# Retention, mixer and gated layers in one kernel: loads four steps ahead, stores a slot later, weights fetched one per item

## The chip, the cores and the metric

The kernel runs on one core of a Trainium2 chip. The core has TensorE (PE, the matrix engine), VectorE (DVE), ScalarE (ACT), GpSimd (POOL) and SyncE (SP); in this kernel SP issues every DMA, in the order in which they are written. The metric is the device time of one execution in microseconds (us), as the median of several runs. The profile shows one execution.

## The reference

Three layers follow one another on 8 sequences of 576 positions, all in float32:

```python
# 1. retention: q, k, v are [8, 8 heads, 576, 64]
gamma = 1.0 - 2.0 ** (-5.0 - np.arange(H))
Dmat = np.where(rel >= 0, gamma[:, None, None] ** rel[None], 0.0)    # rel = i - j
attn = np.matmul(scale * np.matmul(q, k.T) * Dmat, v)                # x is [8, 576, 512]
# 2. mixer
h = x.transpose(0, 2, 1) @ U @ V                                     # rank 32, along the sequence
u = x + h.transpose(0, 2, 1)
x = u + np.maximum(u @ w_ch1, 0.0) @ w_ch2                           # 512 -> 2048 -> 512
# 3. gated layer
x_prev = x shifted by one position
xk = mu_k * x + (1 - mu_k) * x_prev;  xr = mu_r * x + (1 - mu_r) * x_prev
out = sigmoid(xr @ w_r) * (np.maximum(xk @ w_k, 0.0) ** 2 @ w_v)     # 512 -> 1024 -> 512
```

## The kernel before

The 4608 positions (8 sequences of 576) are cut into 9 blocks of 512 columns. Every large product is made in the number format fp32r, of which one operand alone is not exact enough: each operand is split into a high and a low part (ACT copies the high part, DVE or POOL subtracts it), and PE makes three products, high by high, low by high and high by low. Pairs of products of halves are made in seven instead of eight (the Strassen-Winograd scheme), for which sums and differences of weight quarters and of data quarters are made ahead. Weights arrive as 64-bit floats and are converted on the chip by ACT (`high`, `low`) and DVE (`join`).

**Stage 1, retention, and the first half of the mixer.** 40 steps, 5 for each of the 8 sequences ("batches" below), work through the chunks of a sequence (`step_of`, L1218). A step scales the keys of the step after next on POOL (`scale_k`, L796), makes the retention products on PE (`products_of`: `inter` L867, `own` L886, and for the next step `scores` L834 and `gain` L908), leaves PSUM by DVE (L848, L933, L945, L962), and transposes the result (L972). What a step loads (`load`, L787 qk and L789 kv, 512 KB each) is fetched by `load_to` at its start. The low-rank products (L993) and the mixing product (`mix`, L1023, added to the data by DVE at L1027) follow some steps later; in the third step of a batch they are done between parts of the hidden blocks.

Between retention products PE makes "hidden blocks": u by `w_ch1`, 128 rows for one block of columns (`hidden_part`, L381, 3 parts of 4 matmuls; ACT's relu L387 and a store L392 follow). A hidden block needs one of nine small tiles and one of two PSUM banks.

Beside that, `slot()` runs jobs in stages, one stage per slot: the weights of later stages are loaded (L184, L221, L224), converted, summed, split (ACT L132 and L270, POOL L133 and L271) and stored to DRAM (L193, L277), and one entry of the list `sums` (L1168) is taken per slot: the first sums of `w_ch1` for the pair below (`first_sums`, L290: DVE L298 and L306 to L309, ACT L314, DVE L315, store L316).

Loads, weights and operands share the pool `big` of 35 buffers of 4 KB per partition; a load waits on SP until its buffer is free, and everything behind it on SP waits too. The order of work is written out by hand: every engine does its instructions in the order of the program.

At the end of the stage the last hidden blocks are made (L1271) while ACT and DVE make the operands of the pair (`operands`, a generator whose steps are taken by `next`).

**Stage 2, the first product of the last pair of blocks** (`first_group`, L1294 on, matmuls L1327, 8 groups of 7 products). Its sums come back from DRAM by `load_first` (L327), one group ahead, into the pool `big2` of 16 buffers. `tick` runs a slot four times in a group; the second weights 0 to 3 are converted in these slots (`second_weight`, loads L412, activations L100 and L104, casts L449).

**Stage 3, the second product** (`products`, matmuls L552): 64 items, 16 for each pair of blocks. An item loads its hidden rows four items ahead (`load_item`, L481 to L484), makes sums two items ahead (`sums_item`, L492 to L496, one stored at L494) and splits one item ahead (`split_item`, ACT L511, DVE L512). The second weights 4 to 7 were stored in stage 1 and are loaded by `load_second` (L466).

**Stage 4, the gated layer**, follows.

Of the kernel before, what the change touches and what calls it, by code (L numbers as in the profile page):

```python
# [9 lines left out]
F32 = mybir.dt.float32  # L10
F32R = mybir.dt.float32r
# [32 lines left out]
def retention_mixer_kernel(ctx: ExitStack, tc: tile.TileContext, io):  # L44
# [15 lines left out]
    def unit(pool, dt, nm):  # L60
        return pool.tile([128, 2, 512], dt, tag="unit", name=nm)
# [36 lines left out]
    def high(out, raw):  # L98
        w = raw.bitcast(U32).rearrange("p (n t) -> p n t", t=2)
        nc.scalar.activation(out, w[:, :, 1].bitcast(F32), AF.Prelu, scale=DOWN, alpha=NEGATIVE)  # L100

    def low(out, raw):
        w = raw.bitcast(U8).rearrange("p (n t) -> p n t", t=8)
        nc.scalar.activation(out, w[:, :, 3], AF.Copy, scale=TOP, bias=BELOW)  # L104
# [184 lines left out]
    def first_sums(g):  # L289
        got = {}  # L290

        def whole():
            got["x"] = [cv.tile([128, 512], F32, tag="cf", name="cf", bufs=5) for _ in range(2)]
            for i, x in enumerate(got["x"]):
                f = g + HF * i
                w, c = w1[f // 4], slice((f % 4) * 128, (f % 4 + 1) * 128)
                for k in range(2):
                    nc.vector.tensor_tensor(  # L298
                        x[:, 256 * k:256 * k + 256].rearrange("p (k n) -> p k n", n=128),
                        w.h[k][:, :, c].bitcast(F32), w.l[k][:, :, c].bitcast(F32), op=ALU.add,  # L300
                    )

        def sums():
            x, y = got["x"]
            a11, a12, a21, a22 = x[:, :256], x[:, 256:], y[:, :256], y[:, 256:]
            nc.vector.tensor_tensor(a22, a21, a22, op=ALU.add)  # L306
            nc.vector.tensor_tensor(a21, a11, a21, op=ALU.subtract)
            nc.vector.tensor_tensor(a11, a22, a11, op=ALU.subtract)
            nc.vector.tensor_tensor(a12, a12, a11, op=ALU.subtract)  # L309

        def part(i):
            x = got["x"][1 - i]
            y = unit(big, F32R, f"fs{g}_{i}")
            nc.scalar.copy(y[:, 0], x)  # L314
            nc.vector.tensor_tensor(y[:, 1], x, y[:, 0].bitcast(F32), op=ALU.subtract)  # L315
            nc.sync.dma_start(  # L316
                kept_1[g][:, i], y.bitcast(F32).rearrange("p l (s n) -> p l s n", n=256)
            )

        return [whole, sums, lambda: part(0), lambda: part(1)]  # L320

    fs = {}

    def load_first(g):
        for i in range(2):
            x = fs[g, i] = big2.tile([128, 2, 2, 256], F32R, tag="unit", name=f"fw{g}_{i}")
            nc.sync.dma_start(x.bitcast(F32), kept_1[g][:, i])  # L327

    wkp, wkq = {}, {}
# [74 lines left out]
    def second_weight(j, pool):  # L404
        raw, got = [], {}
        out = pool if j else big2

        def load():
            for i in range(2):
                r = big2.tile([128, 512], I64, tag="unit", name=f"w2raw{j}_{i}")  # L410
                f = j + 8 * i
                nc.sync.dma_start(r, io["moe_w_ch2"][f * 128:(f + 1) * 128, :])  # L412
                raw.append(r)

        def down():
            got["a"] = unit(big2, F32, f"w2a{j}")
            got["f"] = unit(big2, F32, f"w2f{j}")
            for i in range(2):
                high(got["a"][:, i], raw[i])
                low(got["f"][:, i].bitcast(U32), raw[i])  # L420

        def fill(i):
            f = got["f"][:, i]
            join(f, got["a"][:, i], f.bitcast(U32))

        def sums():
            x = got["s"] = big2.tile([128, 4, 256], F32, tag="unit", name=f"w2s{j}")
            f = got["f"]
            a11, a21, a12, a22 = f[:, 0, :256], f[:, 0, 256:], f[:, 1, :256], f[:, 1, 256:]
            s1, s3, s2, s4 = (x[:, i] for i in range(4))  # L430
            eng = nc.gpsimd
            eng.tensor_tensor(s1, a21, a22, op=ALU.add)
            eng.tensor_tensor(s2, s1, a11, op=ALU.subtract)
            eng.tensor_tensor(s3, a11, a21, op=ALU.subtract)
            eng.tensor_tensor(s4, a12, s2, op=ALU.subtract)

        def part(i, lo, eng):
            w = (wp, wq)[i]
            if j not in w:
                w[j] = [  # L440
                    out.tile([128, 4, 256], F32R, tag="unit", name=f"w2{'pq'[i]}{j}_{x}")
                    for x in range(2)
                ]
            if lo:
                src = got["s"][:, 2 * i:2 * i + 2]
            else:
                src = got["f"][:, :, 256 * i:256 * i + 256]
            h, l = (x[:, 2 * lo:2 * lo + 2] for x in w[j])
            nc.scalar.copy(h, src)  # L449
            eng.tensor_tensor(l, src, h.bitcast(F32), op=ALU.subtract)  # L450

        def parts(lo, eng):
            for i in range(2):
                part(i, lo, eng)

        return [
            load, None, down, lambda: fill(0), lambda: fill(1), sums,
            lambda: parts(0, nc.vector), lambda: parts(1, nc.gpsimd),
        ]

# [304 lines left out]
    with ExitStack() as st:  # L765
# [395 lines left out]
        jobs += [block_weight(j, big, io["moe_w_ch2"], kept_2, "s", True) for j in range(KEPT, HF)]  # L1161
        for at, job in zip((0, 2, 4, 6, 8, 10, 12, 14, 16, 17), jobs):
            waiting.insert(at, job)
        sums = [x for g in range(HF) for x in first_sums(g)]

        def load_to(n):
            while units and N - len(units) < n:
                load(*units.pop(0))  # L1168
# [46 lines left out]

        def step_of(i):
            b, p = seq[i]
            load_to(i + (4 if i < 2 * NC else 3))  # L1218
            if i + 2 < N:
                scale_k(*seq[i + 2])  # L1220
            for fn, args in first.pop(i, []):
# [47 lines left out]
        gen = operands(x1, 0, even, odd, "f")  # L1269
        next(gen)  # L1270
        while ready:  # L1271
            hidden(1)
            for _ in range(3):
                next(gen, None)
        for _ in gen:
            pass
# [12 lines left out]

    def tick():  # L1290
        ticks.append(0)
        slot(new=len(ticks) % 4 == 1)

    exits = []  # L1294

# [57 lines left out]

        exits.append(last)

    load_first(0)
    for g in range(HF):
        extra = {}
        if g + 1 < HF:
# [9 lines left out]
        first_group(g, 4 * (g % 2), extra)  # L1369
    while exits:  # L1370
        exits.pop(0)()
    for j in range(KEPT, HF):
        load_second(j, 0)
    for n, (q, h, j) in enumerate(ITEMS):
        if n + 4 < len(ITEMS):
            load_item(n + 4)
        if n + 2 < len(ITEMS):
            sums_item(n + 2)
        if n + 1 < len(ITEMS):
            split_item(n + 1)  # L1380
        if j > 5:
            load_rest(q, ((0, 3), (2, 1))[h][j - 6])
        if n >= len(ITEMS) - 4:
            load_hidden(n - len(ITEMS) + 4)
        if n == len(ITEMS) - 1:
            split_hidden(0)
        if n and n % 2 == 0 and n < 2 * (HF - KEPT) + 1:
            load_second(KEPT + n // 2 - 1, 1)
        products(n)
        slot()  # L1390
        for _ in range(2):
            if rest and j < NF // 2 - 1:
                rest.pop(0)()
# [272 lines left out]
```

## Time and profile before

| | |
|---|---|
| median of 3 runs | 1434.05 us (1430.72 to 1437.57) |
| profiled execution | 1433.46 us, span 1431.7 us |
| PE busy | 1352.3 us, 94% of the span, 10248 matmuls |
| DVE, ACT, POOL busy | 912.7, 678.3, 376.8 us |
| granted clock of PE, mean | 0.970 |
| DMA | 342.11 MB, mean 239 GB/s, 67.3% of the 16 engines' span |

Times count from the first instruction. Busy is the time in which an engine works on an instruction; the idle time before an instruction is put down to what released it. The granted clock is the share of TensorE's full clock, 2.4 GHz; 0.50 is its lower level, 1.2 GHz, and a value between is the mean of a stretch. The DMA share is the mean busy share of the 16 DMA engines.

### The profile page before, as it was taken

How to read it: one execution, taken by the hardware profiler on the slowest of the kernel's cores; microseconds unless marked ns; L12 is line 12 of the kernel's file. 1: busy time of each engine (PE TensorE's matmuls, PEld its weight loads, DVE VectorE, ACT ScalarE, POOL GpSimd, SP SyncE). 2: the span in 40 equal slices, each digit the busy share in tenths (PEclk: the TensorE clock that was granted, in tenths of full speed). 3: DMA queues.
4: the chain of work that ended last, by engine and by line, in shares of the span. 5: the costliest groups of instructions: out<-in, count | busy, mean ns of one | idle time of the engine just before them, and what ended most of it. 6: DMA issues, size and time to landing. Idle time of an engine off the chain costs nothing.

```text
span 1431.7 us, 26130 instructions
## 1 busy us (share of the span) xinstructions
PE 1352.3 (94%) x10248; PEld 1105.8 (77%) x10248; DVE 912.7 (64%) x1268; ACT 678.3 (47%) x1185; POOL 376.8 (26%) x317
## 2 busy tenths in 40 slices
PE   6999888898998979979999999999999999999998
PEld 4688766676776767768788888888888888888897
DVE  4544465545433145467979798888797788787753
ACT  5553444445433237644434444465455455465432
POOL 2340244243443004202222221211411403303312
PEclk8899999999999999999999999999999999999999
DMA  9666698889886357898969888589147066074172
GB/s 346 229 212 233 236 324 290 299 309 331 284 270 210 130 180 261 292 375 312 316 225 307 278 281 284 193 308 349 70 164 279 29 231 239 1 266 175 70 288 84
DMA packets 134827, 342.11 MB, mean 239 GB/s; under 512 B 16432, under 2 KB 29616, under 8 KB 134704
## 3 DMA queue, kind: packets, MB, share of 16 engines
q1 hardware_dynamic: 134704, 340.44, 67.3%
q8 instruction: 81, 1.33, 0.4%
q14 instruction: 42, 0.34, 0.1%
HBM read 232.38 MB, written 108.00 MB: 238 GB/s over the span
## 4 chain that ended last, share of the span: by engine, by line
PE 58%; DMA 2%; DVE 1%; ACT 1%; issue 1%; SPq 0%; POOL 0%; DVEq 0%; ACTq 0%
PE v L1511 14%; PE gc L552 6%; PE ga L552 6%; PE gd L552 6%; PE kd L1415 3%; PE kc L1415 3%; PE ka L1415 3%; PE gb L552 2%; PE kb L1415 2%; PE rd L1415 2%; PE rc L1415 2%; PE ra L1415 2%; PE fc L1327 1%; PE fa L1327 1%; PE fd L1327 1%; PE c L633 1%
## 5 line engine op out<-in xcount | busy, mean ns | idle before, releaser
L387 ACT ACTIVATE hs<-h 128x512 f32<-128x512 f32 x112 | 66.7, 597 | 179.8 <-PE h L381 174.6
L1467 POOL TENSOR_TENSOR vl<-m,vh 128x512 fp32r<-128x512 f32 (+1 forms) x40 | 47.6, 1192 | 310.2 <-ACT vh L1466 240.2
L796 POOL TENSOR_TENSOR kv<-kv,ktab 128x512 f32<-128x512 f32 (+1 forms) x40 | 38.4, 959 | 231.7 <-DMA kv<-in_kv 155.2
L511 ACT CAST sbh<-rb 128x1024 fp32r<-128x1024 f32 x64 | 67.3, 1052 | 50.3 <-PE gd L552 39.2
L1511 PE MATMUL v<-vh,wv_0u 128*128 128x512 f32 x288 | 88.7, 389 | 0.0
L1511 PE MATMUL v<-vh,wv_1u 128*128 128x512 f32 x288 | 88.6, 389 | 0.0
L512 DVE TENSOR_TENSOR sbl<-rb,sbh 128x1024 fp32r<-128x1024 f32 x64 | 85.1, 1329 | 3.8 <-ACT sbh L511 3.6
L511 ACT CAST sah<-ra 128x1024 fp32r<-128x1024 f32 (+1 forms) x64 | 53.5, 836 | 66.7 <-DVE ra L493 29.9
L512 DVE TENSOR_TENSOR sal<-ra,sah 128x1024 fp32r<-128x1024 f32 (+1 forms) x64 | 65.2, 1018 | 25.1 <-ACT sah L511 12.9
L1467 POOL TENSOR_TENSOR vl<-c,vh 128x512 fp32r<-128x512 f32 (+1 forms) x40 | 62.1, 1573 | 25.9 <-ACT vh L1466 25.9
L1027 DVE TENSOR_TENSOR xt<-mx,xt 128x256 f32<-128x256 f32 x64 | 28.7, 457 | 61.7 <-PE mx L1023 61.7
L315 DVE TENSOR_TENSOR fs<-cf,fs 128x512 fp32r<-128x512 f32 x16 | 14.7, 922 | 81.2 <-ACT fs L314 73.2
L848 DVE TENSOR_TENSOR pm<-up,dtab 128x512 f32<-128x512 f32 (+1 forms) x40 | 25.3, 633 | 64.3 <-PE up L834 58.7
L1511 PEld LDWEIGHTS v<-vh,wv_1u 128*128 128x128 f32 x288 | 54.1, 188 | 11.2
L1511 PEld LDWEIGHTS v<-vh,wv_0u 128*128 128x128 f32 x288 | 53.9, 188 | 11.0
L1466 ACT CAST vh<-m 128x512 fp32r<-128x512 f32 (+1 forms) x40 | 23.2, 579 | 75.3 <-DVE m L1465 75.3
L1511 PE MATMUL v<-vl,wv_0u 128*128 128x512 f32 x144 | 56.0, 389 | 0.0
L1511 PE MATMUL v<-vl,wv_1u 128*128 128x512 f32 x144 | 56.0, 389 | 0.0
L569 POOL TENSOR_TENSOR m<-m,ur 128x512 f32<-128x512 f32 x8 | 11.7, 1490 | 162.9 <-ACT m L566 162.9
L596 POOL TENSOR_TENSOR x<-x,ur 128x512 f32<-128x512 f32 x16 | 24.6, 1549 | 106.5 <-DVE x L592 51.5
L665 ACT ACTIVATE tp<-x2l,omu 128x511 f32<-128x511 f32 x72 | 50.9, 712 | 3.3 <-DMA x2l<-xb 3.3
L1465 DVE SCALAR_TENSOR_TENSOR m<-m 128x512 f32<-128x512 f32 (+1 forms) x40 | 44.8, 1119 | 1.4
(375 smaller groups left out, 3983.3 us busy)
## 6 DMA issues: line engine op xcount, KB each, us to landing
wk<-keys SPq DMA_DIRECT2D x80, 512.0 KB, 5.8
rb<-hp SPq DMA_DIRECT2D x64, 512.0 KB, 6.9
hp<-hs SPq DMA_DIRECT2D x112, 256.0 KB, 3.6
wr<-gates SPq DMA_DIRECT2D x40, 512.0 KB, 6.7
qk<-in_qk SPq DMA_DIRECT2D x32, 512.0 KB, 6.0
kv<-in_kv SPq DMA_DIRECT2D x32, 512.0 KB, 6.6
ra<-hp SPq DMA_DIRECT2D x32, 512.0 KB, 7.0
ur<-ub SPq DMA_DIRECT2D x18, 512.0 KB, 5.6
```

Of the source, the lines that this page charges most:

```text
L387: nc.scalar.activation(h, hps.pop((t, f)), AF.Relu)
L511: nc.scalar.copy(hi_, src)
L512: nc.vector.tensor_tensor(lo_, src, hi_.bitcast(F32), op=ALU.subtract)
L552: nc.tensor.matmul(group[g][p], l[:, col(p)], r, start=(h == 0 and j == 0 and i == 0), stop=(i == 2 and last), skip_group_check=True,)
L665: nc.scalar.activation(tp[:, 1:], x[:, :BT - 1], AF.Copy, scale=omu[:, j, k:k + 1])
L796: nc.gpsimd.tensor_tensor(k, k, ktab[:, p, :n].to_broadcast([128, n, NP, D]), op=ALU.mult)
L1027: nc.vector.tensor_tensor(u, ps[:, :n], u, op=ALU.add)
L1327: nc.tensor.matmul(ps[b], w(lo, i), x[:, i], start=(new and i == 0 and j == 0), stop=(i == 1 and j == 2), skip_group_check=True,)
L1415: nc.tensor.matmul(ps[b], l, r[:, i], start=(part == 0 and i == 0 and j == 0), stop=(i == 1 and j == 2), skip_group_check=True,)
L1465: nc.vector.scalar_tensor_tensor(x, x, 0.0, x, op0=ALU.max, op1=ALU.mult)
L1467: eng.tensor_tensor(l, x, h.bitcast(F32), op=ALU.subtract)
L1511: nc.tensor.matmul(vacc[t][o], w.part(lo, g, col(o)), x[:, i, :], start=(g == 0 and i == 0 and j == 0), stop=(g == NG - 1 and i == 1 and j ...
```

## The change

Five things are done. The retention fetch runs four steps ahead in all steps (before, three from the eleventh on). The store of a first sum becomes a stage of its own, a slot behind the stage that makes it, and the last store of a group shares its stage with the first sum of the next group, so that the list has 41 entries instead of 32. The first sums of group 0 come into the pool `big` and are loaded before the last three hidden blocks, and the operand generator takes a step behind each part of a block. A second weight is converted a word per stage (9 stages instead of 8), and a new one starts every 6 ticks instead of 4. The kept second weights are loaded one per item, the first halves in items 0 to 3 and the second in items 6 to 9.

```diff
@@ first_sums
         def part(i):
             x = got["x"][1 - i]
-            y = unit(big, F32R, f"fs{g}_{i}")
+            y = got[i] = unit(big, F32R, f"fs{g}_{i}")
             nc.scalar.copy(y[:, 0], x)
             nc.vector.tensor_tensor(y[:, 1], x, y[:, 0].bitcast(F32), op=ALU.subtract)
+
+        def store(i):
             nc.sync.dma_start(
-                kept_1[g][:, i], y.bitcast(F32).rearrange("p l (s n) -> p l s n", n=256)
+                kept_1[g][:, i], got[i].bitcast(F32).rearrange("p l (s n) -> p l s n", n=256)
             )
 
-        return [whole, sums, lambda: part(0), lambda: part(1)]
+        return [whole, sums, lambda: part(0), lambda: store(0), lambda: part(1), lambda: store(1)]
@@ load_first
-            x = fs[g, i] = big2.tile([128, 2, 2, 256], F32R, tag="unit", name=f"fw{g}_{i}")
+            x = fs[g, i] = (big2 if g else big).tile([128, 2, 2, 256], F32R, tag="unit", name=f"fw{g}_{i}")
@@ second_weight
-            for i in range(2):
-                high(got["a"][:, i], raw[i])
-                low(got["f"][:, i].bitcast(U32), raw[i])
+
+        def words(i):
+            if i == 0:
+                down()
+            high(got["a"][:, i], raw[i])
+            low(got["f"][:, i].bitcast(U32), raw[i])
...
-            load, None, down, lambda: fill(0), lambda: fill(1), sums,
+            load, None, lambda: words(0), lambda: words(1), lambda: fill(0), lambda: fill(1), sums,
@@ the list of first sums
-        sums = [x for g in range(HF) for x in first_sums(g)]
+        sums = []
+        for g in range(HF):
+            x = first_sums(g)
+            if sums:
+                before, begin = sums[-1], x[0]
+                sums[-1] = lambda before=before, begin=begin: (before(), begin())
+                x = x[1:]
+            sums.extend(x)
@@ step_of
-            load_to(i + (4 if i < 2 * NC else 3))
+            load_to(i + 4)
@@ the last hidden blocks
         while ready:
-            hidden(1)
-            for _ in range(3):
+            if len(ready) == 3:
+                load_first(0)
+            t, f = ready.pop(0)
+            for part in range(3):
+                hidden_part(t, f, part)
                 next(gen, None)
@@ tick
-        slot(new=len(ticks) % 4 == 1)
+        slot(new=len(ticks) % 6 == 1)
@@ ahead of the groups, and of the items
-    load_first(0)
...
-    for j in range(KEPT, HF):
-        load_second(j, 0)
@@ the items
-        if n and n % 2 == 0 and n < 2 * (HF - KEPT) + 1:
-            load_second(KEPT + n // 2 - 1, 1)
+        if n < HF - KEPT:
+            load_second(KEPT + n, 0)
+        elif n >= HF - 2 and n - HF + 2 < HF - KEPT:
+            load_second(KEPT + n - HF + 2, 1)
         products(n)
```

## Rows read from the trace of the kernel before

**Rows 1.** Windows: length; busy PE, PEld, DVE, ACT, POOL; clock, DMA share, GB/s.
```profile
136.00:202.60 66.60, 62.25 (x815) 49.63 (x809) 34.04 (x62) 30.94 (x59) 21.34 (x21) 0.95 0.76 267
202.60:277.30 74.70, 63.59 (x824) 51.07 (x819) 38.24 (x63) 33.37 (x65) 27.29 (x25) 0.93 0.85 297
277.30:348.80 71.50, 63.61 (x820) 50.92 (x813) 35.29 (x69) 31.19 (x60) 27.32 (x26) 0.93 0.87 309
348.80:419.00 70.20, 63.00 (x816) 50.85 (x808) 27.61 (x44) 32.43 (x62) 29.28 (x28) 0.93 0.84 296
419.00:471.40 52.40, 44.09 (x644) 35.53 (x637) 13.72 (x28) 14.60 (x30) 17.76 (x17) 0.90 0.64 218
...
609.60:650.00 40.40, 32.49 (x132) 25.72 (x131) 26.55 (x33) 16.70 (x19) 0.00 (x0) 0.92 0.98 380
650.00:1374.00 724.00, 722.46 (x3184) 596.88 (x3183) 586.09 (x714) 361.86 (x581) 176.61 (x116) 1.00 0.62 217
```

**Rows 2.** Windows of single retention steps, and of the fourth to second steps.
```profile
85.70:94.10 8.40, 8.40 (x180) 6.91 (x173) 3.42 (x7) 6.01 (x12) 4.88 (x4) 1.00 0.24 93
102.50:115.00 12.50, 12.50 (x196) 10.15 (x191) 6.21 (x13) 2.34 (x5) 1.46 (x2) 1.00 0.33 108
136.00:147.40 11.40, 11.39 (x188) 9.03 (x182) 8.15 (x18) 4.94 (x10) 0.80 (x1) 1.00 0.76 263
256.30:277.30 21.00, 21.00 (x274) 17.01 (x267) 9.94 (x18) 11.59 (x23) 5.71 (x4) 1.00 0.95 332
277.30:295.70 18.40, 13.73 (x188) 10.87 (x181) 5.46 (x14) 5.06 (x10) 8.01 (x9) 0.81 0.95 328
...
461.10:471.40 10.30, 10.30 (x130) 8.31 (x124) 2.38 (x5) 2.79 (x7) 0.00 (x0) 1.00 0.60 175
181.00:232.30 51.30, 46.38 (x619) 37.31 (x615) 27.14 (x46) 25.86 (x51) 21.59 (x20) 0.93 0.94 320
256.30:307.30 51.00, 46.14 (x620) 36.95 (x614) 23.70 (x48) 25.81 (x51) 17.28 (x15) 0.93 0.91 316
327.40:378.50 51.10, 46.29 (x624) 37.21 (x617) 24.48 (x36) 26.28 (x51) 19.90 (x17) 0.93 0.92 329
```

**Rows 3.** PE's waits from 140 to 460 us: total, times, longest (us).
```profile
PE dn L908 <- POOL kv L796: 17.5, 11, 2.7
PE up L834 <- DMA qk<-in_qk: 13.4, 6, 3.0
PE mx L1023 <- DVE xt L1027: 5.7, 2, 4.9
PE mx L1023 <- ACT xs L982: 2.1, 1, 2.1
```

**Rows 4.** SP's waits from 120 to 460 us.
```profile
SPq L316 <- DVE fs L315: 28.5, 11, 4.5
SPq L787 <- POOL wsl L271: 12.8, 2, 6.6
```

**Rows 5.** POOL's waits from 140 to 460 us.
```profile
POOL kv L796 <- DMA kv<-in_kv: 110.8, 15, 16.8
```

**Rows 6.** Timeline of PE, opening a batch: start, us, instruction, idle before it.
```profile
280.69 0.69 PE L834 MATMUL up<-qk 64*64 64x64 f32 x32 [2.77 <-DMA qk<-in_qk]
```

**Rows 7.** Timeline of PE at the end of the hidden blocks.
```profile
512.32 1.20 PE L381 MATMUL h<-uh,w_3h 128*128 128x512 f32 x4 [1.29 <-ACT hs L387]
...
528.60 0.80 PE L1327 MATMUL fc<-fht,fw 128*128 128x512 f32 x1 [5.00 <-DMA fw<-first]
```

**Rows 8.** Timeline of ACT there.
```profile
510.72 1.05 ACT L697 CAST fht<-xt 128x1024 fp32r<-128x1024 f32 x1 [3.57 <-DVE xt L701]
```

**Rows 9.** PE's waits from 530 to 608 us, stage 2.
```profile
PE fa L1327 <- ACT f L1333: 3.0, 2, 1.5
```

**Rows 10.** Timeline of SP at the first items.
```profile
615.93 4.66 SPq L466 DMA_DIRECT2D w2p<-second  x8
```

**Rows 11.** Timeline of PE at the fifth item.
```profile
635.11 0.80 PE L552 MATMUL ga<-sal,w2p 128*128 128x512 f32 x1 [6.20 <-DVE sal L512]
```

## The prediction

> **What bounds the kernel now.** I read the windows by stage first [rows 1]. From 650 us to 1374 TensorE (PE) works 722.46 of 724.00 us at the full clock of 2.4 GHz (granted 1.00), so nothing that the change does can shorten that part, and nothing won ahead of it is given back there: what ends earlier before 650 moves the end by as much. The losses lie ahead of it. One batch of the retention stage takes 66.6, 74.7, 71.5 and 70.2 us for batches 3 to 6, and the last one (four of its five steps) 52.4, at granted clocks of 0.90 to 0.95.
>
> Single steps give the measure [rows 2]. The step that opens a batch takes 11.4 us at clock 1.00 (136.0 to 147.4, 188 matmuls) and 18.4 us where it is disturbed (277.3 to 295.7, the same 188 matmuls, clock 0.81): PE idles 4.7 us in it and then runs for a while at 1.2 GHz, half of its clock. The second step of a batch has the same matmuls as the first (11.4). The third is the 12.5 of 102.5 to 115.0 with one more hidden block of 12 matmuls, 2.7 us at its pace: 15.2. The fourth and fifth together take 21.0. An undisturbed batch is so 11.4 + 11.4 + 15.2 + 21.0 = 59.0 us, and the four steps of the last, with fewer hidden blocks, 8.4 + 8.4 + 12.5 + 10.3 = 39.6. The five stretches last 335.4 us and hold 4 x 59.0 + 39.6 = 275.6 of work: 59.8 us are lost.
>
> The waits of PE in that stage say what is late [rows 3]: 17.5 us (11 times) for POOL's scaling of kv, 13.4 (6 times) for the qk transfer itself, 5.7 and 2.1 for the mixing product. The clock loss that follows each gap is not in these sums. POOL's scaling waits for its own transfer, 110.8 us [rows 5], and blocks POOL's queue meanwhile; the 4.9 us wait of a mixing product hangs on that too, by a DVE sum that needs a buffer which POOL frees. So the fetch of qk and kv, issued one step before use, comes some 3 us late about twice a batch ([rows 6] is one). SP's queue is the reason [rows 4]: it stands 28.5 us (11 times) before the stores of the first sums until DVE has made them, and 12.8 us (twice) before a qk load until POOL frees a buffer.
>
> **The change, part by part.**
>
> *Fetch one step earlier, stores a slot later.* No transfer is added in the stage: the same qk, kv and fs DMAs, each pair of loads moved up in SP's queue by one step (8 to 15 us) past that step's hidden stores, weight loads and weight stores; the fs stores go one slot back, so SP's 28.5 us go. A lead of one step covers every wait of [rows 3], whose longest is 4.9 us. Behind the loads on SP stand the hidden stores; POOL has its scaling ready a step early, and its splits, the stores that wait for them, and DVE's sums come sooner. The first sums now need 41 slots instead of 32 (5 per group, the last store joined with the next group's first sum) and run on into the last two batches, where the DMA has room (0.64 in the last stretch of [rows 1]).
>
> What is late next is the DMA. From a batch's fourth step to the second of the next its share is 0.94, 0.91 and 0.92 over 51.3, 51.0 and 51.1 us [rows 2], of which 43.8 are work (21.0 + 11.4 + 11.4). The best that a long stretch of this trace reaches is 0.98, from 609.6 to 650 us [rows 1]. At that the three stretches need 49.2, 47.4 and 48.0 us: 5.4 + 3.6 + 4.2 = 13.2 us of the loss stay. So 59.8 - 13.2 = 46.6. I take off 6 for the gap in batch 3 [rows 3] (PE on ACT xs, 2.1, with the clock loss after it), where ACT is busy with casts and no fetch is late. Value: **40 us**. Bounds: 59.8 if the extra lead carries the surplus into the light third steps, and below nothing if the buffers don't allow the lead (rivals).
>
> The Trainium skill, page "DMA: Bandwidth & Descriptors", section Specifications, gives a core's share of HBM as about 358 GB/s. By that rule batches 4 and 5 (297 x 74.7 = 22.2 MB and 22.1 MB) would need 62.0 and 61.7 us, the retention stage would give 48 instead of 40, and the item stretch below 2 us less than I put down: 1374 in all. The trace does not follow it: 380 GB/s in one stretch of [rows 1], and 320 to 329 at over 0.9 busy in those of [rows 2].
>
> *End of the hidden blocks.* PE waits 5.00 us for the first sums' transfer [rows 7], which is issued only after the last hidden store; now it is issued three blocks (8 us) earlier from the other pool, where PE needs nothing else. That gives 5.0. The finer interleaving of the operand casts with the three parts of a block works against it: ACT's cast of ft waits for DVE until 510.72 [rows 8], and the relu behind it already holds PE for 1.29 us [rows 7]. With one generator step per part instead of three per block, two further casts of 1.05 us come ahead of that same relu, and PE's wait there grows by 2.1. Sum: **3 us** (0 to 8).
>
> *Second weights made a word at a time, a new one every 6 ticks instead of 4.* PE waits twice for ACT, 3.0 us in all [rows 9], where two words (four activations) and two casts of the weight before fall in one tick. Now one word does. I take **2 us**; 0 to 3. The last weight starts at tick 19 and ends at 27 of 32, ahead of its first use: nothing is late.
>
> *Kept second weights one per item.* SP issues eight 512 KB loads at once, 4.66 us, and the fifth item's operands behind them [rows 10]; PE then waits 6.20 us for a difference of these operands [rows 11]. The clock of that stretch is 0.92 over 40.4 us [rows 1], so up to 3.2 us more are lost to it. The change puts the item's loads first and two weight loads behind them. Is the DMA then late? Four items with 2 x 0.52 MB of operands, 0.26 of store and 1.05 of weights move 9.4 MB, which at 380 GB/s takes 24.8 us against 21.8 of PE work (24 matmuls each, at 227 ns: 722.46 us over 3184): 3 us behind after four items, and operands are fetched two items (10.9 us) ahead of their sums. It is covered. The second halves go from items 2, 4, 6, 8 to items 6 to 9, where the first use is item 12. **8 us**; 0 to 9.4.
>
> Sum: 40 + 3 + 2 + 8 = 53. The profiled execution took 1433.5 us (span 1431.7), 0.6 under the median of the runs, 1434.05, so the forecast is **1380 us**.
>
> **The rivals.**
>
> *The buffers eat the lead.* The pool has 35 buffers, and by my count of the code 35 are held at some loads now; two more per step can't be had, so the load of step i + 3 has to wait for a buffer of step i. In the likely case that is one that PE frees within about 1 us of the step's start. For this rival speaks that qk loads already stand up to 6.6 us for POOL [rows 4]. If POOL's buffers are what is waited for, most of the lead goes; what stays is the 28.5 us off SP and the other three parts: 13 + about 8 = 21, so 1412.
>
> *Slower: SP held longer than the lead.* Same place, another price: everything that SP does is in order, so a held load holds the hidden stores, these hold the nine small tiles, these hold ACT's relu and PE's banks. It decides at a hold of about 11 us a step; at 13 us in some 20 steps it costs 2 us each, 40 in all, less 13 from the other parts: 1460. Against it: the two holds seen are 6.4 us on average, and an earlier kv ends POOL's 110.8 us of waiting, so POOL frees sooner.
>
> *The DMA is no limit.* The surplus drains in the light third steps and every loss goes, the gap in batch 3 too: 1433.5 - 59.8 - 13 = 1361.
>
> *Nothing changes* because another wait of the same size stands right behind each: against this speaks that undisturbed steps run at clock 1.00 with no gap [rows 2].
>
> **Chances.** Forecast 0.60 (its own range 1366 to 1396); buffers eat the lead 0.18; no DMA limit 0.08; slower 0.08; nothing 0.06. The range from 1362 to 1416 takes in the forecast, most of the first rival and a part of the third. Over 0.5% is 7 us, about what a measurement of this kernel can tell: faster 0.86, within it 0.06, slower 0.08.
>
> **What would show it.** PE's waits for POOL kv and qk under 5 us together in the retention stage; batches of 60 to 65 us; DMA share over 0.95 from fourth to second steps; no SP wait on the sums; POOL's wait for kv gone. At the end of the hidden blocks no wait for fw, but one of 3 to 4 us for a relu. No PE gap over 1 us at the fifth item. The prediction is wrong if qk loads wait on SP for POOL in most steps, or if PE waits for hidden relus in the retention stage.

## The result, and the profile after

The changed kernel takes 1443.41 us (median of 9 runs, 1438.67 to 1447.46), the kernel before 1434.05 in the same rounds: a ratio of 1.0063, interval 1.0045 to 1.0080. It is slower by 9 us, where 1380 was forecast. The profiled execution took 1441.68 us, its span 1439.9.

Windows of the profile after, batch by batch (length; busy PE, PEld, DVE, ACT, POOL with instructions; clock, DMA share, GB/s):

```profile
136.40:206.40 70.00, 61.81 (x820) 49.66 (x812) 32.74 (x57) 29.54 (x56) 22.54 (x21) 0.95 0.69 233
206.40:298.90 92.50, 67.13 (x808) 52.59 (x809) 32.60 (x58) 32.78 (x63) 27.62 (x25) 0.87 0.68 238
298.90:369.90 71.00, 63.87 (x804) 50.92 (x808) 38.52 (x61) 31.58 (x60) 31.71 (x30) 0.93 0.90 313
369.90:453.20 83.30, 64.50 (x820) 51.03 (x814) 33.52 (x61) 32.78 (x62) 25.57 (x24) 0.90 0.71 251
453.20:493.20 40.00, 40.00 (x652) 32.61 (x646) 14.64 (x29) 15.99 (x33) 17.29 (x16) 1.00 0.85 299
620.00:650.00 30.00, 27.90 (x113) 21.89 (x113) 22.06 (x27) 15.23 (x18) 0.00 (x0) 0.94 1.01 378
```

Against [rows 1] the last batch is what was forecast (40.0 us, no gap, clock 1.00; 52.4 before), and around the start of the items, at 630.8 us, PE works 27.90 of 30.00 us at a clock of 0.94 (last line above). But the batches before it take 70.0, 92.5, 71.0 and 83.3 us instead of 66.6, 74.7, 71.5 and 70.2. The five stretches last 356.8 us; before they lasted 335.4, and 295 was forecast. PE's waits in the retention and the last hidden blocks, 140 to 530 us, have changed altogether (total, times, longest):

```profile
PE h L383 <- ACT hs L389: 29.9, 8, 9.0
PE mx L1028 <- ACT xs L987: 12.7, 3, 8.1
PE mx L1028 <- DVE xt L1032: 10.6, 4, 6.7
PE up L872 <- ACT w L936: 3.1, 1, 3.1
PE up L872 <- DVE y L950: 2.5, 1, 2.5
```

The waits for qk and for POOL's kv of [rows 3], 30.9 us together, are gone. In their place PE waits for ACT: for the relu that ends a hidden block (29.9 us; 2.6 us in the same window before) and for the copy ahead of the mixing product (12.7 instead of 2.1). ACT's waits in the same stretch say why:

```profile
ACT wkf L104 <- POOL wkl L271: 15.9, 3, 8.9
ACT wsf L104 <- POOL wsl L271: 13.6, 2, 7.5
ACT fs L314 <- PE up L872: 7.8, 2, 5.3
ACT wsh L270 <- DMA first<-fs: 6.7, 2, 4.8
ACT wrh L270 <- PE up L872: 4.8, 1, 4.8
ACT fs L314 <- DMA second<-wsl: 4.8, 2, 4.5
```

In none of these does the releaser make what ACT reads. POOL's split wkl is no input of a conversion of the next weight; it is the last reader of the buffer that this conversion writes. Each line is a wait for one of the 35 buffers of the pool `big`. Summed over the conversions and splits of ACT (L104, L132, L270, L314, L370; those that write the small `cf` tiles left out) that waited for a store, for PE's last read or for POOL's split, it comes to 78.4 us in 23 waits. Before, the same sum is 2.4 us in 2:

```profile
ACT wv_0p L132 <- POOL wkl L271: 2.0, 1, 2.0
ACT fs L314 <- POOL wkl L271: 0.4, 1, 0.4
```

One wait of the changed kernel, followed through the timelines of SP, POOL, ACT and PE (start, length, instruction, idle before it and releaser):

```profile
218.19 0.34 SPq L792 DMA_DIRECT2D qk<-in_qk  x1
227.99 0.34 SPq L794 DMA_DIRECT2D kv<-in_kv  x1
230.29 1.13 SPq L277 DMA_DIRECT2D keys<-wkh  x2
...
236.54 2.48 POOL L271 TENSOR_TENSOR wkl<-wkf,wkh 128x512 fp32r<-128x512 f32 x2 [15.98 <-DMA keys<-wkh]
...
239.06 0.66 ACT L104 ACTIVATE wkf<-wkraw 128x512 uint32<-128x512 uint8 x1 [8.87 <-POOL wkl L271]
...
244.08 1.09 ACT L389 ACTIVATE hs<-h 128x512 f32<-128x512 f32 x2
...
244.74 1.65 PE L383 MATMUL h<-uh,w_2h 128*128 128x512 f32 x3 [8.99 <-ACT hs L389]
```

SP holds a kv load from 218.5 to 228.0 until PE frees a buffer; the store of wkh stands behind it. POOL's split waits 16.0 us for that store to free its buffer, ACT's conversion 8.9 us for the buffer that the split reads, two relus stand behind the conversion on ACT (after 4.4 us of other work that was held too), and PE idles 9.0 us. SP's waits after, 140 to 530 us:

```profile
SPq L794 <- PE up L872: 15.6, 2, 9.4
SPq L794 <- PE h L383: 14.7, 1, 14.7
SPq L184 <- ACT wkf L104: 13.1, 3, 5.2
SPq L794 <- DMA first<-fs: 9.1, 3, 4.0
```

The wait of the stores for DVE's sums [rows 4] is gone, as forecast; loads that wait for a buffer stand there instead, 63.3 us for all qk and kv loads (before 16.6). POOL's wait for its kv [rows 5] has fallen from 110.8 to 2.8 us.

Outside the retention it went as forecast. PE's timeline at the end of the hidden blocks and in the items:

```profile
536.21 1.20 PE L383 MATMUL h<-uh,w_3h 128*128 128x512 f32 x4 [3.51 <-ACT hs L389]
...
572.06 0.50 PE L1342 MATMUL fc<-fht,w_2h 128*128 128x512 f32 x1 [0.74 <-ACT f L1348]
...
602.67 0.50 PE L1342 MATMUL fc<-fht,w_3h 128*128 128x512 f32 x1 [1.50 <-ACT f L1348]
...
632.04 0.73 PE L557 MATMUL ga<-sah,w2p 128*128 128x512 f32 x2 [1.24 <-ACT sah L516]
```

The wait for fw [rows 7] is gone and the relu's has grown to 3.51 us. From that relu to the first item it is 98.1 us (532.7 to 630.8; before 511.0 to 615.3, 104.3), and from there to the end 809.1 (before 816.4): 6.2 and 7.3 us won. Up to that relu 21.7 us are lost.

### The profile page after: what moved, and what is told of

Its sections match the earlier page's. It is cut to its first block, busy times and chain, and to the rows that moved or that the text cites. A ratio compares the mean times of both kernels' runs of the same rounds, so it can differ in the third digit from the quotient of the medians.

```text
span 1439.9 us, 26131 instructions
## 1 busy us (share of the span) xinstructions
PE 1350.4 (94%) x10248; PEld 1103.1 (77%) x10248; DVE 915.8 (64%) x1268; ACT 677.3 (47%) x1185; POOL 379.8 (26%) x317
## 4 chain that ended last, share of the span: by engine, by line
PE 70%; DMA 5%; DVE 4%; ACT 2%; issue 2%; SPq 1%; POOL 1%; DVEq 0%; ACTq 0%; POOLq 0%
PE v L1525 13%; PE h L383 11%; PE gc L557 6%; PE ga L557 6%; PE gd L557 6%; PE kd L1429 3%; PE kc L1429 3%; PE ka L1429 3%; PE gb L557 3%; PE kb L1429 2%; PE rd L1429 2%; PE rc L1429 2%; PE ra L1429 2%; PE c L639 1%; PE c L638 1%
## 5 line engine op out<-in xcount | busy, mean ns | idle before, releaser
L517 DVE TENSOR_TENSOR sal<-ra,sah 128x1024 fp32r<-128x1024 f32 (+1 forms) x64 | 66.6, 1040 | 20.3 <-PE gd L557 12.2
L1032 DVE TENSOR_TENSOR xt<-mx,xt 128x256 f32<-128x256 f32 x64 | 28.7, 456 | 56.8 <-PE mx L1028 56.7
L383 PE MATMUL h<-uh,w_2h 128*128 128x512 f32 x112 | 35.2, 440 | 27.9 <-ACT hs L389 27.9
```

Of the source, the lines that this page charges most:

```text
L383: nc.tensor.matmul(hps[t, f], w.part(lo, k, fo), u[k // 2][:, k % 2, :], start=(part == 0 and k == 0), stop=(part == 2 and k == KD - 1),)
L517: nc.vector.tensor_tensor(lo_, src, hi_.bitcast(F32), op=ALU.subtract)
L1032: nc.vector.tensor_tensor(u, ps[:, :n], u, op=ALU.add)
```

## The experiments

**First question: which of the two retention edits costs?** Theory A: fetch and later stores together overfill the 35 buffers, so that ACT's own conversions wait for one and the relus behind them are late. Theory B: loads on SP wait for buffers and hold the hidden stores behind them. Theory C: what costs is the later stores and the 41 slots themselves. The letters are used again further down, with a meaning of their own in each group. Four kernels:

The change with the fetch of before:

```diff
-            load_to(i + 4)
+            load_to(i + (4 if i < 2 * NC else 3))
```

> The changed kernel with the fetch three steps ahead again; all else of the change stays. Theory A (buffers on ACT): the lead of four and the stores a slot later together hold more than the 35 buffers, so conversions on ACT wait for a buffer and the hidden relus behind them come late; without the lead the pool fits, PE's 29.9 us of waits for relus in the retention stage go, the fetch waits of before come back in part: about 1418 us (1410 to 1426). Theory B (buffers on SP): loads that wait for a buffer hold the hidden stores on SP, and those the relus; here too they go: about 1420. Theory C (stores and first sums): the stores a slot later and the 41 slots of sums bunch the work of ACT and DVE; the relu waits stay: 1440 or more.

1437.72 us, ratio 1.0015 (0.9999 to 1.0032). SP's waits for DVE's sums are gone here too, and the fetch is still late. PE's waits, 140 to 530 us:

```profile
PE up L839 <- DMA qk<-in_qk: 17.0, 5, 6.0
PE dn L913 <- POOL kv L801: 10.9, 7, 1.9
```

The kernel before with the fetch alone:

```diff
-            load_to(i + (4 if i < 2 * NC else 3))
+            load_to(i + 4)
```

> The kernel before with the fetch four steps ahead in all steps as the only edit. Theory A: the loads exceed the pool and wait on SP for buffers of their own step, but hardly an allocation on ACT does; the waits for qk and kv go and few relu waits come: 1400 to 1425. Theory B: SP is held by the loads as in the changed kernel, relus late: 1445 to 1460 (the changed kernel without the gains at the end of the stage and in the items). Theory C: no stores moved, so the lead gives all it can: about 1393.

1419.03 us, ratio 0.9891 (0.9855 to 0.9927).

The kernel before with two buffers of `big` held through the retention; DVE sets one column of each at the start and the end:

```diff
+        held = [unit(big, F32, f"held{k}") for k in range(2)]
+        for x in held:
+            nc.vector.memset(x[:, 0, 0:1], 0.0)
         for i in range(N):
             step_of(i)
+        for x in held:
+            nc.vector.memset(x[:, 0, 0:1], 0.0)
```

> The kernel before, fetch three ahead, with two of the 35 buffers held idle through the retention stage. Same number of free buffers as with the lead of four, without the lead. Theory A: few allocations on ACT exceed 33, loads come a little later: 1436 to 1448. Theory B: the loads on SP wait and hold the stores: 1445 to 1465. Theory C: the pool does not matter: 1434 within 4.

1460.94 us, ratio 1.0184 (1.0147 to 1.0221): 25 us for two buffers, with nothing else moved. That lies in theory B's range and 13 us above theory A's, but the trace has the waits where theory A puts them: ACT's waits for a buffer are 39.7 us (2.4 in the kernel before), SP's at qk and kv loads 14.4 us (16.6).

The change with each store back in its part's stage, and so 32 entries:

```diff
-        return [whole, sums, lambda: part(0), lambda: store(0), lambda: part(1), lambda: store(1)]
+        return [whole, sums, lambda: (part(0), store(0)), lambda: (part(1), store(1))]
...
-        sums = []
...
+        sums = [x for g in range(HF) for x in first_sums(g)]
```

> The changed kernel with each store of a first sum back in the stage of its part and 32 entries in the list; the fetch four ahead, the end of the stage, the ticks and the items as changed. Theory A: without the later stores ACT's allocations fit again; the lead works: 1385 to 1412. Theory B: the loads still wait on SP: 1436 to 1448, as the changed kernel. Theory C: 1380.

1401.61 us, ratio 0.9775 (0.9744 to 0.9806): it beats both kernels. The later stores, with the 41 entries that came with them, cost 41.8 us beside the fetch of four. Theory B, for which the fetch alone should have lost and this kernel too, falls. Theory A holds for the second and fourth kernel; it misses the first by 20 us (the store edit costs with a fetch of three, too) and puts the price of two buffers in the third too low.

**Second question: is it the later store or the longer list?** Theory H says the longer hold, theory S the spacing of the entries. First, 33 entries with each store a slot later; then, 41 entries with each store in its part's stage:

```diff
-        return [whole, sums, lambda: part(0), lambda: store(0), lambda: part(1), lambda: store(1)]
+        return [whole, sums, lambda: part(0), lambda: (store(0), part(1)), lambda: store(1)]
```

```diff
-        return [whole, sums, lambda: part(0), lambda: store(0), lambda: part(1), lambda: store(1)]
+        return [whole, sums, lambda: (part(0), store(0)), lambda: None, lambda: (part(1), store(1)), lambda: None]
```

> The changed kernel, but the list of first sums has 33 entries instead of 41: each store still goes a slot behind its part, the first store of a group shares a slot with the second part, the second store with the next group's first sum. Theory H (what costs is that each sum holds its 4 KB buffer, and its place in SP's queue, a slot longer): near the changed kernel, 1428 to 1445 us. Theory S (what costs is the spacing of 41 entries, which puts DVE's long sums at other places of the steps and runs them on into later batches): near the kernel with the store in its part's stage, 1396 to 1412.

1413.67 us, ratio 0.9859 (0.9839 to 0.9880).

> The changed kernel with its 41 entries, but each store issued in its part's stage and an empty stage where the store was; the sums and parts stand at the same slots as in the changed kernel. Theory H: near the kernel with the store in its part's stage, 1396 to 1412 us. Theory S: near the changed kernel, 1428 to 1445.

1415.67 us, ratio 0.9875 (0.9849 to 0.9902). Neither theory alone: from 1401.6 the later store costs 12.1, the spacing 14.1, both 41.8. They don't just add; together they cost 15.6 more.

The kernel with 32 entries and the stores with their parts is called the short-list kernel from here. It was run with the fetch of before, so that only the three parts behind the retention are left of the change, and with one empty entry ahead of the list:

```diff
-            load_to(i + 4)
+            load_to(i + (4 if i < 2 * NC else 3))
```

```diff
-        sums = [x for g in range(HF) for x in first_sums(g)]
+        sums = [lambda: None] + [x for g in range(HF) for x in first_sums(g)]
```

> The kernel before with only the edits behind the retention: group 0 of the first sums loaded before the last hidden blocks, a word of a second weight per stage, the kept second weights one per item. My sum had 3 + 2 + 8 = 13 us for these: 1421 (1418 to 1425). Theory H and theory S both say so; if it comes out at 1434 or above, the loss of the fetch-of-three kernel does not lie in the store edit at all.

1417.84 us, ratio 0.9886 (0.9865 to 0.9907): 17.2 us for the three parts (13 forecast). The fetch of four is then worth 16.2 (1417.8 to 1401.6), and 17.0 on the kernel before.

> The kernel with the store in its part's stage (four entries per group), with one empty entry ahead of the list: every first sum stands one slot later, so that DVE's four long additions go to the other half of a step; nothing is held longer. Theory H: as without the shift, 1397 to 1407 us. Theory S (the place of the sums in the step decides): 10 us or more away from 1401.6, either way.

1412.57 us, ratio 0.9854 (0.9830 to 0.9878). Shifted by one slot, with nothing held longer by the code, the list costs 11 us. That spoke for theory S; the traces show what the shift does: ACT's first sums wait for a buffer there, 16.5 us for the store of the sum before and 6.6 for PE.

**Third question: loads or places of work?** Theory P: the early loads take the buffers. Theory Q: the places of DVE's and ACT's work decide. Fetch moved behind the products of a step, in the changed and in the short-list kernel; and the four long additions of a first sum cut into two and two:

```diff
-            load_to(i + 4)
...
             products_of(i)
+            load_to(i + 4)
...
-        def whole():
+        def whole(i):
...
         def sums():
+            whole(1)
```

> The changed kernel, but the fetch of step i + 4 is issued behind the products of step i instead of at its start: a lead of about three and a half steps, with a buffer of step i freed ahead of it in the program. By a count of the code the loads that find all 35 buffers held fall from 22 to 6, those of conversions and splits stay. Theory P (the pool: loads of the long lead take or wait for the buffers that conversions need): 1405 to 1425 us. Theory Q (the places of the DVE and ACT work of the first sums in a step decide, whatever the pool): 1432 to 1447.

1443.28 us, ratio 1.0055 (1.0035 to 1.0076).

> The kernel with the store in its part's stage, and the fetch of step i + 4 behind the products of step i: no load finds all 35 buffers held any more by the count (17 before), 13 splits and conversions still do. Theory P: faster than 1401.6 us, 1385 to 1398. Theory Q: 1398 to 1406.

1404.12 us, ratio 0.9778 (0.9743 to 0.9813).

> The kernel with the store in its part's stage, and the four long additions of a first sum (6.3 us of DVE in a row at one place of the trace, ahead of the retention's own work) cut into two of 3 us, the second two with the four short ones of the next stage. Theory P: within 4 us of 1401.6. Theory Q: 1385 to 1397.

1405.41 us, ratio 0.9792 (0.9766 to 0.9819).

> Both: fetch of step i + 4 behind the products of step i, and the long additions halved, with the store in its part's stage. If both theories have a part, below each of the two: 1378 to 1392 us; if only one, as that one.

1403.49 us, ratio 0.9782 (0.9754 to 0.9811). All four stand within 4 us of the kernel that they start from. Theory P misses the first two, theory Q the third: moving the loads, or halving DVE's long additions, changes nothing here. That doesn't clear the pool, since the first two left its waits as they were: in the changed kernel the count of held buffers in program order fell for the loads from 22 to 6, but SP's loads waited 65.6 us for buffers (63.3 without the move) and ACT 75.0 (78.4). Such a count is a poor guide.

**Fourth question: the wait for a buffer on ACT (theory B here), or the slots (theory C)?** On the short-list kernel: one buffer held as above; each first sum's buffer kept two slots longer by a DVE write of one column, its store where it was; and the weight jobs started four in nine slots, there and in the changed kernel (the calls of `keep`, two entries behind each part, are left out below):

```diff
+        def keep(i):
+            nc.vector.memset(got[i][:, 0, 0:1].bitcast(F32), 0.0)
```

```diff
-                    slot(new=len(quiet) % 2 == 1 or len(quiet) > 40)
+                    slot(new=len(quiet) % 9 in (1, 3, 5, 7) or len(quiet) > 40)
```

> The kernel with the store in its part's stage, with one of the 35 buffers of the pool held idle through the retention (DVE sets one column of it at the start and at the end); nothing else is moved. Theory B (what costs is a conversion on ACT that waits for a buffer, with the hidden relus queued behind it): ACT's waits for buffers grow and the time with them, 1412 to 1435 us. Theory C (the slot at which the first sums' work and stores stand): within 5 us of 1401.6.

1456.29 us, ratio 1.0154 (1.0118 to 1.0189): one buffer of 35 costs 54.7 us, more than theory B said and far from theory C. ACT's waits of that kernel, 140 to 530 us, look like those of the change, though its list and stores are the short ones:

```profile
ACT wkf L104 <- POOL wkl L271: 20.9, 3, 8.7
ACT wsf L104 <- POOL wsl L271: 15.5, 2, 9.4
...
ACT wv_1p L132 <- DMA gates<-wrh: 8.1, 1, 8.1
ACT wv_1p L132 <- PE up L872: 5.8, 1, 5.8
```

and PE's longest wait in it is again for the relu:

```profile
PE h L383 <- ACT hs L389: 40.1, 8, 10.5
```

> The kernel with the store in its part's stage and 32 entries, but each first sum's buffer kept two slots longer by a DVE write of one column behind its store; the store itself stays where it is in SP's queue. Theory B: like the kernel whose 33 entries store a slot later, 1409 to 1422 us. Theory C (there it was the store's place in SP's queue): 1399 to 1406.

1413.62 us, ratio 0.9855 (0.9826 to 0.9885): what the later store costs with 33 entries (1413.67), without moving a store. SP's waits for DVE's sums are 39.0 us here and 0.7 with 33 entries, at the same time. So the hold is what costs there, and neither the store's place in SP's queue nor SP's wait.

> The changed kernel, all of it, but the weight jobs of the retention start four in nine slots instead of one in two, so that fewer of their buffers are held at a time and the last jobs end in the last batch; by the count of the code the conversions on ACT that find all buffers held fall from 14 to 5. Theory B: ACT's waits for buffers and PE's for relus fall, 1408 to 1430 us. Theory C: first sums and stores stand where they stood, 1436 to 1448.

1420.40 us, ratio 0.9908 (0.9873 to 0.9943), in theory B's range: 23 us back, with first sums and stores where the change has them.

> The kernel with the store in its part's stage, with weight jobs starting four in nine slots: no conversion on ACT finds all buffers held by the count (6 before). Theory B: faster than 1401.6 us, 1384 to 1397. Theory C: 1398 to 1407.

1411.51 us, ratio 0.9842 (0.9808 to 0.9876): a miss for both, 10 us slower than the short-list kernel. The other spacing makes ACT's first sums meet buffers that come free late (L314 waits 12.0 us for PE and 12.2 for stores); ACT's sum rises from 29.8 to 43.6 us. Like the kernel before with two buffers held, this run tells ACT's waits from SP's: its loads wait on SP no longer than those of the short-list kernel (15.2 against 17.8 us). But the weight jobs' work stands at other slots in it too.

**A better version.** The weight blocks' stores treated as the first sums' are in the short-list kernel, each in the stage of its split; and then the additions halved as well:

```diff
-            load, None, down, lambda: fill(0), lambda: fill(1), sums, lambda: parts(0),
-            lambda: store(0), lambda: parts(1), lambda: store(1),
+            load, None, down, lambda: fill(0), lambda: fill(1), sums,
+            lambda: (parts(0), store(0)), lambda: (parts(1), store(1)),
```

> The kernel with the first sums' stores in their part's stage, and the weight blocks' stores treated the same way: each is issued in the stage of its split and not a slot behind, so that two stages and the slots for which two pairs of buffers are held go. By the count of the code 33 buffers are held at most conversions and loads instead of 34 and 35, and 8 of them find all 35 held instead of 30. Theory B: ACT's waits for buffers fall, 1385 to 1398 us, less if SP's added waits for POOL's splits (1.3 to 1.7 us each) hold the hidden stores: up to 1408. Theory C: 1395 to 1410, by the new slots of the jobs.

1402.53 us, ratio 0.9794 (0.9767 to 0.9822), which lies in the ranges of both theories and decides nothing between them. ACT's waits for buffers fell to 13.3 us, of which these are most, and SP's for POOL's splits, which the edit was to add, came to little (waits of ACT, then of SP):

```profile
ACT wv_1p L132 <- DMA first<-fs: 4.9, 2, 2.6
ACT wv_0p L132 <- DMA first<-fs: 3.7, 2, 3.3
...
SPq L277 <- POOL wkl L271: 6.9, 12, 0.8
SPq L277 <- POOL wsl L271: 5.4, 10, 1.1
```

Its median is not below that of the short-list kernel, and its runs spread more (1396.3 to 1406.5).

> All stores of the stage issued with their parts, and the four long additions of a first sum (now 3.8 us of DVE in a row ahead of the retention's own work, behind which PE waited 5.9 us for a mixing sum) cut into two and two. Theory B says nothing of it: 1397 to 1407 us. Theory C (the place of DVE's work): 1385 to 1396.

1395.58 us, ratio 0.9734 (0.9711 to 0.9756): the fastest, 38 us under the kernel before. Its interval overlaps that of the short-list kernel (0.9744 to 0.9806), so that its lead over that one is likely and not shown. It came out in theory C's range, with its interval below that of the kernel without the halving (0.9767 to 0.9822), though single runs of the two overlap. So the place of DVE's additions, which was worth nothing in the short-list kernel, is likely to be worth some 7 us once the pool has room.

**All together.** For each kernel with the fetch of four and the three later parts, from 140 to 530 us: ACT's waits for a buffer (summed as above), SP's waits at qk and kv loads, and the median:

| kernel | ACT, us | SP, us | median, us |
|---|---|---|---|
| all stores at once | 13.3 | 5.1 | 1402.5 |
| all stores at once, additions halved | 15.4 | 6.3 | 1395.6 |
| short list, additions halved | 26.5 | 19.1 | 1405.4 |
| short list, fetch mid-step, additions halved | 28.3 | 17.2 | 1403.5 |
| short list, fetch mid-step | 28.9 | 18.7 | 1404.1 |
| short list | 29.8 | 17.8 | 1401.6 |
| short list, one slot on | 42.9 | 29.1 | 1412.6 |
| short list, slower jobs | 43.6 | 15.2 | 1411.5 |
| 33 entries, stores later | 45.4 | 40.1 | 1413.7 |
| 41 entries, stores with parts | 46.8 | 27.5 | 1415.7 |
| the change, slower jobs | 48.2 | 33.2 | 1420.4 |
| short list, kept two slots longer | 48.5 | 37.8 | 1413.6 |
| the change, fetch mid-step | 75.0 | 65.6 | 1443.3 |
| short list, one buffer held | 76.5 | 72.7 | 1456.3 |
| the change | 78.4 | 63.3 | 1443.4 |

From 29.8 us up the time goes with ACT's waits: some 0.9 us for each us of them (from 29.8 to 78.4 it is 41.8 us for 48.6). Between 42.9 and 48.5 us on ACT the time stays within 9 us, while SP's holds run from 15.2 to 40.1. Below 29.8 us it goes with them no longer (13.3 us at 1402.5). In the three slowest kernels SP's holds are high as well, 63 to 73 us, and no run parts the two there. The waits are those of the profiled execution, which for the first two rows took 1396.3 and 1402.8 us and not the median.

PE's side of the sum: between the profiled executions of the change and of the short list (spans 1439.9 and 1402.2) PE idles 28.7 us more and works 9.0 us longer on the same 10248 matmuls (busy 1350.4 against 1341.4, mean granted clock 0.970 against 0.977).

## Why the prediction was wrong

**The step that failed** is the first of the part by part, the stores a slot later: "the fs stores go one slot back, so SP's 28.5 us go", with no price on the other side. The wait on SP did go, but the fetch came no earlier for it: in the change with the fetch of before, PE still waits 27.9 us for qk and kv (29.0 in the three later parts alone). In the short-list kernel the wait is back at 20.7 us (12 times), while PE waits for no fetch. What the edit buys it with is one slot more for each of 16 sums' buffers, and with the 41 entries another order in which buffers come free. In a pool with none to spare the two together cost 41.8 us: 12.1 for the later store, which the kernel with the longer hold shows, 14.1 for the spacing, which goes with 17 us more of ACT's waits, and the rest where they meet. I had counted that 35 of 35 were held "at some loads", and looked for the price at the loads alone; ACT's conversions take their buffers from the same pool, and the relus queue behind them.

**The second failure is a size.** The fetch a step earlier, with the stores, was put at 40 us, and alone it gives 16 to 17. The first half of its mechanism is right: the qk and kv waits are gone in every kernel with it. But the lead takes two buffers more, and ACT's waits rise from 3.2 to 29.8 us (the three later parts alone against the short list), so that PE waits for relus and mixing sums instead. PE's waits of the short-list kernel, 140 to 530 us:

```profile
PE h L383 <- ACT hs L389: 23.4, 9, 7.0
PE mx L1028 <- DVE xt L1032: 8.1, 3, 5.6
PE mx L1028 <- ACT xs L987: 6.5, 2, 4.0
```

The next limit was to be the DMA, with 49.2, 47.4 and 48.0 us for the fourth to second steps. The same stretches of the short-list kernel:

```profile
184.00:238.20 54.20, 45.91 (x618) 36.41 (x612) 29.33 (x45) 25.61 (x50) 26.24 (x23) 0.94 0.91 312
260.70:314.40 53.70, 45.81 (x622) 36.30 (x616) 26.62 (x45) 25.80 (x51) 22.04 (x20) 0.94 0.95 325
331.70:379.60 47.90, 45.14 (x624) 36.38 (x618) 20.82 (x37) 26.72 (x51) 24.65 (x23) 0.96 0.99 351
```

Only the third comes to its forecast, at a share of 0.99. In the first two what PE waits for is ACT's relus alone (8.3 and 7.9 us), at shares of 0.91 and 0.95. The forecast's ceiling was also read too low, as the last section shows, and the slowest of the three stretches of [rows 2] moves 316 GB/s, not 320. The gap in batch 3, for which 6 us were left out of the gain, stayed (3.8 us in the change, 4.0 in the short-list kernel).

**What held.** End of the hidden blocks and second weights: 3 + 2 forecast, 6.2 measured between the two traces, with the relu's wait at 3.51 us where 3 to 4 was said. In part that is luck: of the 6.2 us only 3.8 are idle time of PE, and 2.4 are busy time saved at the higher clock (0.97 before, 1.00 after), which the forecast did not count; the wait for the second weights fell only from 3.0 to 2.2 us, where a gain of 2 was forecast. Kept second weights one per item: 8 forecast, 7.3 measured, the gap at the fifth item gone. The three parts alone came to 17.2 us in the medians against 13; in that kernel's own trace the spans give 2.4 us up to the last relu, 4.2 to the first item and 8.6 behind it, 15.2 in all. POOL's wait for kv [rows 5] fell as said.

**The rivals.** "Slower: SP held longer than the lead" named the end of the chain rightly, relus and then PE, and the sign; so did the last sentence of the prediction, that it is wrong if PE waits for hidden relus. Its road was only half right. Held loads on SP do start single chains, as the one shown, but over the kernels the time goes with ACT's own waits, and two runs have these without the holds on SP. Its time, 1460, was too high by 17, and it had been given a chance of 0.08. "Buffers eat the lead" was wrong in its price: the lead was there (no qk or kv wait), and the buffers took it elsewhere.

**What stays open.** The change with the fetch of before is 20 us slower than the three later parts alone (1437.7 against 1417.8), with ACT's waits up by only 15.8 us (3.2 to 19.0); part of it stands in waits of ACT for the small buffers of the sums, 14.4 us, which were not tried by themselves. PE's waits are 8.8 us longer there; those ahead of mixing products alone grow from 8.2 to 17.7 us. How the later store and the spacing come to cost 15.6 us more together was not tried either. And the kernels were compared with waits summed in one execution each; which single buffer costs most was not tried.

## What to carry to other kernels

Before moving a store back by a slot to spare a queue a wait, ask what the buffer that it frees is worth: in a pool without spare, one buffer of 35 cost 55 us here, and a wait of SP for a store's data, 39.0 us or 0.7, made no difference. Read the waits of every engine that allocates from a full pool, not only of the one that loads: here each releaser that is no producer of the instruction's input was a wait for a buffer, and what matters is what stands behind it in that engine's order. And price two edits that draw on the same pool together: the later store and the longer list cost 12 and 14 us apart, together 42.

## What the runs showed that was not expected

The forecast took 380 GB/s [rows 1] as the best that the transfers of a long stretch reach. But that is the mean of 40.4 us whose start is slower: from 620 to 650 us the kernel before already moves more (first line, columns as above), and the kernel with the three later parts alone does so while PE has no gap at all (second line):

```profile
620.00:650.00 30.00, 23.80 (x96) 19.22 (x95) 17.73 (x21) 10.00 (x10) 0.00 (x0) 0.89 1.03 412
620.00:650.00 30.00, 30.00 (x134) 24.86 (x133) 21.05 (x23) 12.83 (x17) 3.66 (x3) 1.00 1.03 413
```

The Trainium skill, page "Perfetto Trace Analysis", section "Roofline", says that the 358 GB/s which the prediction weighed is the share of a core when both cores of a pair draw on it, and that one core alone can go above it, to about 435. With one core at work this case's 413 agrees.

The same page of the Trainium skill, "Perfetto Trace Analysis", section "Optimization Strategy", says that a gap which keeps coming back on the engine that should be full can mean that there is no room for the next tile. This case agrees, with a turn: the room was missing on ACT (78.4 us), and on PE it showed as waits for relus (29.9 us), which need no buffer of that pool.
